# One store over the rows of two batches in an attention and gated FFN kernel

## The chip, the cores and the metric

The kernel runs on 1 core of one Trainium2 chip. The metric is the device time of one execution in microseconds (us), taken as the median of several runs. The engines are TensorE (PE, with PEld for its weight loads), VectorE (DVE), ScalarE (ACT), GpSimd (POOL) and SyncE (SP); 16 DMA engines serve the core. SP issues all loads of the attention's inputs, all DMA transposes and all stores, in one in-order queue; POOL issues the nine loads of the FFN weights.

## The reference

Causal attention over 8 batches, 8 heads and 576 positions with 16 extra "beacon" keys and values ahead of each sequence, then an FFN with a gated hidden layer over the 4608 rows of its output:

```python
k_all = np.concatenate([beacon_k, k], axis=2)        # (8, 8, 592, 64)
v_all = np.concatenate([beacon_v, v], axis=2)
scores = scale * np.matmul(q, k_all.transpose(0, 1, 3, 2))
scores = np.where(causal, -1000000000.0, scores)
a = np.exp(scores - scores.max(-1, keepdims=True))
a /= a.sum(-1, keepdims=True) + 1e-09
x = (a @ v_all).transpose(0, 2, 1, 3).reshape(4608, 512)
gate = np.maximum(x @ w_gate, 0.0)                   # w_gate, w_val: 512 x 1536
out = gate * (x @ w_val) @ w_out                     # w_out: 1536 x 512, out: 4608 x 512
```

Inputs and output are float32; the products are made in bf16 on PE.

## The kernel before

**Attention, by batch.** For each batch SP loads q, k, v and the beacons into staging tiles `st` (7 buffers, lines 520, 562 and 594 to 597). POOL scales and rounds them to bf16 (`h` at line 486, `v` at line 442), PE turns `h` with four small matmuls (line 497), and ACT or DVE copies the turned rows into `kT` and `diag`. Scores are matmuls of `diag` with `kT` (lines 655 to 663), DVE finds the row minima (line 678), ACT takes the exponential (line 689), POOL divides by the sums (line 710), a DMA transpose on SP's queue turns the probabilities (`pTb<-pb` and `pTf<-pf`, line 756), and PE multiplies them with the values (lines 766 and 795). The result goes transposed into `xT`.

**FFN, by 512 rows.** `hidden` makes the two products of line 833 for each of 12 blocks of hidden units, ACT takes the ReLU of the gate (line 837), and DVE multiplies (line 841). `project` makes one tile of 128 output rows: 12 matmuls at line 853 in three parts, a copy from PSUM to a tile `osb` (4 buffers) by ACT or DVE (lines 438 and 440), and the store on SP's queue (line 865).

**The rows that the change is about.** Each batch has 576 rows, 512 of which go through the FFN by themselves, with four stores of 128 rows. The 64 rows that remain of each batch are collected: those of batches 0 to 3 make one group, those of batches 4 to 7 another. In such a group a tile of 128 output rows holds 64 rows of one batch and 64 of the next, which lie 576 rows apart in the output. The first group is worked on in the middle of the kernel; its two tiles are stored at 236.9 and 242.0 us. The second group comes last. Its first tile is 512 columns wide, its second is made as two halves of 256 columns (`LAST_PARTS = 2`), so the last three tiles of the kernel are of this kind.

**The order of the work.** Nothing in the kernel waits by the order of the source. Every step is a task with a cost, a priority and the buffers that it holds; `Plan.order` plays the tasks through with these costs and emits them one by one, each engine's instructions in the order that the planner reached them. A DMA task has a cost of `(issue, move)`: how long it takes SP's queue to issue it and how long it takes to move. The tile framework adds the semaphores. So a task less, or another cost, can change the order of all that the planner emits after it.

Of the kernel before, what the change touches and what calls it, by code (L numbers as in the profile page):

```python
# [51 lines left out]
OUT = -1300.0  # L52
# [93 lines left out]
class Plan:  # L146
# [7 lines left out]
    def add(self, engines, cost, run, deps=(), holds=(), prio=0.0, lag=None, part=False, lazy=0.0, after=0.0, move=0.0):  # L154
        t = Task(engines if isinstance(engines, tuple) else (engines,), cost, run, deps, holds, prio, lag, part, lazy, move)
        t.ready = after
        for d in t.deps:
            d.users.append(t)
        self.tasks.append(t)
        return t  # L160
# [107 lines left out]
def kernel(  # L268
# [12 lines left out]
    nc = tc.nc  # L281
    B, H, S, D = q.shape
# [4 lines left out]
    P = 128  # L287
# [53 lines left out]
    osb_s = outs  # L341
# [7 lines left out]
    f_s, v_ps, first_ps = Share(banks, F_MOST), Share(banks, V_MOST), Share(banks, FIRST_MOST)  # L349
# [3 lines left out]
    add = plan.add  # L353


    def c_dve(n):
        return 0.07 + 0.00104 * n
# [7 lines left out]
    def c_act(n):  # L365
        return 0.06 + 0.00083 * n
# [4 lines left out]
    def c_pe(n):  # L371
        return 0.003 + n / 2400.0
# [63 lines left out]
    def copy(e, dst, src):  # L436
        if e == "ACT":
            nc.scalar.copy(dst, src)  # L438
        elif e == "DVE":
            nc.vector.tensor_copy(dst, src)  # L440
        else:
            nc.gpsimd.tensor_scalar(dst, src, 1.0, 1.0, ALU.mult, ALU.mult)
# [402 lines left out]
    def project(t0, rows, here, hT, prio, last):  # L845
        w = DM // LAST_PARTS if last else DM
        for n0 in range(0, DM, w):
            ps, osb = Hold(f_s, 4), Hold(osb_s, 1 + len(rows))
            prev = None
            for part in range(3):  # L850
                def outp(_, part=part, ps=ps, n0=n0):
                    for nf in range(4 * part, 4 * part + 4):
                        nc.tensor.matmul(ps.tile[:, :w], hT[nf].tile[:, t0:t0 + P], wo_r[:, nf, n0:n0 + w],  # L853
                                         start=(nf == 0), stop=(nf == NF - 1))

                need = [prev, weight_in["o", part]]
                for hid in here:
                    need += hid[4 * part:4 * part + 4] + (hid[:11] if part == 0 else [])
                prev = add("PE", 4 * c_pe(w), outp, need, (ps,) + tuple(hT[4 * part:4 * part + 4]),
                           prio + 0.3 + 0.01 * part + 0.001 * (n0 > 0) - (0.5 if part else 0))  # L860
            ev = add(("ACT", "DVE"), {"ACT": c_act(w), "DVE": c_dve(w)}, lambda x, ps=ps, osb=osb: copy(
                x.engine, osb.tile[:, :w], ps.tile[:, :w]), (prev,), (ps, osb), -1000 + prio)
            at = 0
            for r0, n in rows:
                add("DMA", (0.4, 0.78 * n / P), lambda _, osb=osb, r0=r0, n=n, at=at, n0=n0: nc.sync.dma_start(
                    out[r0:r0 + n, n0:n0 + w], osb.tile[at:at + n, :w]), (ev,), (osb,), prio + OUT)
                at += n


    T0 = 10.0  # L870
# [15 lines left out]
    REG = S // MT * MT  # L886
    for b in range(B):
        hT = [Hold(hid_s, len(CUTS.get(b, ())) + 1 + REG // P) for _ in range(NF)]
        cuts = [0, *CUTS.get(b, ()), REG]
        prio = 1000 + 10.0 * b  # L890
        here = []
        for a, z in zip(cuts, cuts[1:]):
            here.append(hidden(lambda ki, a=a, z=z, b=b: xT[:, ki, b * S + a:b * S + z], z - a, a, done(b, a, z), hT, prio))
            for t0 in range(a // P * P, z // P * P, P):
                project(t0, [(b * S + t0, P)], [x for x, c0, c1 in zip(here, cuts, cuts[1:]) if c0 < t0 + P and c1 > t0],
                        hT, prio, False)
            prio += 2.0
    ends = xT.rearrange("p k (b s) -> p k b s", s=S)
    for i in range(2):
        b0, b1 = i * B // 2, (i + 1) * B // 2  # L900
        w = (b1 - b0) * (S - REG)
        prio = 1000 + 10.0 * b1 - 5.0
        hT = [Hold(hid_s, 1 + w // P + (LAST_PARTS - 1) * i) for _ in range(NF)]
        deps = [x for b in range(b0, b1) for x in done(b, REG, S)]
        hid = hidden(lambda ki, b0=b0, b1=b1: ends[:, ki, b0:b1, REG:], w, 0, deps, hT, prio)
        for t0 in range(0, w, P):
            b = b0 + t0 // (S - REG)
            project(t0, [(x * S + REG, S - REG) for x in (b, b + 1)], [hid], hT, prio, i == 1 and t0 + P == w)
# [37 lines left out]
```

## Time and profile before

| | us |
|---|---|
| median of 3 runs | 409.05 (408.46 to 410.03) |
| the profiled execution | 410.43 |
| its span (first to last instruction) | 408.7 |
| PE busy | 394.1 (96%) |
| DVE, ACT, POOL busy | 315.8, 289.9, 232.7 |

Of the 42 store instructions, 32 carry 128 rows of 2 KB (256 KB), 6 carry 64 rows of 2 KB (128 KB) and 4 carry 64 rows of 1 KB (64 KB). In the profile, an instruction's line is that of the helper that recorded it: 440 and 438 are the copies of all kinds on DVE and ACT, 865 is the store. "SPq" is SP's queue of DMA issues; the time beside an issue is that of issuing, not of the transfer. "To landing" is the time from the start of the issue to the transfer's last semaphore mark.

### The profile page before, as it was taken

To read this page: it belongs to the slowest core of one execution; us is meant where nothing else is said; L and a number is where in the kernel's file an instruction comes from. 1 tells how busy PE (TensorE), PEld (TensorE's weight loads), DVE (VectorE), ACT (ScalarE), POOL (GpSimd) and SP (SyncE) were. 2 spreads that over 40 slices of the span, in tenths; PEclk is the share of its full clock that TensorE was granted. 3 is DMA by queue.
4 is the path that set the end of the run, shared out by engine and by line. 5 is a ranking of instruction groups with operands and counts; after the bars stand their busy time and mean duration, and the time that the engine had idled before them with its cause. 6 is when DMAs were issued, how large, how long until landed. Compare 5 with 4: busy or idle time off the path is not lost.

```text
span 408.7 us, 10376 instructions
## 1 busy us (share of the span) xinstructions
PE 394.1 (96%) x3276; PEld 246.8 (60%) x3311; DVE 315.8 (77%) x1159; ACT 289.9 (71%) x959; POOL 232.7 (57%) x434
## 2 busy tenths in 40 slices
PE   7899999989999999999999999999999999999994
PEld 5567867567766877555557754654554544444483
DVE  6898999889989988899998998787988544244251
ACT  6899989778888968797888799998867432033040
POOL 5899786947777667586975966875727200000000
PEclk9999999999999999999999999999999999999998
DMA  8899999999989999999999999999195730100112
GB/s 224 167 199 225 212 209 196 171 242 219 176 172 230 215 178 231 190 227 195 242 209 210 234 198 189 249 201 205 54 162 125 167 73 0 70 34 0 53 54 51
DMA packets 172616, 68.03 MB, mean 166 GB/s; under 512 B 146832, under 2 KB 168080, under 8 KB 172560
## 3 DMA queue, kind: packets, MB, share of 16 engines
q1 hardware_dynamic: 167808, 62.64, 75.5%
q0 software_dynamic: 4752, 4.72, 7.1%
q8 instruction: 26, 0.43, 0.5%
q14 instruction: 30, 0.25, 0.2%
HBM read 38.27 MB, written 9.44 MB: 117 GB/s over the span
## 4 chain that ended last, share of the span: by engine, by line
PE 84%; POOL 7%; DMA 2%; DVE 2%; ACT 2%; issue 2%; SPq 0%; POOLq 0%
PE f L833 42%; PE f L853 22%; PE f L663 7%; PE f L766 5%; PE f L497 4%; POOL xT L710 2%; POOL pb L710 2%; POOL h L486 2%; PE f L655 2%; DMA st<-in_beacon_k_dram 1%; PE f L795 1%; DMA st<-in_q_dram 1%; DVE diag L440 1%; PE f L745 1%; ACT xT L689 1%
## 5 line engine op out<-in xcount | busy, mean ns | idle before, releaser
L710 POOL TENSOR_SCALAR pb<-pb,small 128x576 bf16<-128x576 bf16 (+8 forms) x224 | 121.6, 557 | 56.0 <-DVE small L703 49.0
L689 ACT ACTIVATE pb<-f,small 128x64 bf16<-128x64 f32 (+6 forms) x256 | 131.0, 524 | 18.0 <-DVE small L678 13.1
L837 ACT ACTIVATE g<-f 128x512 f32<-128x512 f32 (+3 forms) x156 | 71.9, 470 | 67.9 <-PE f L833 66.6
L678 DVE CUSTOM_DVE_ANT_0 f<-f,mask 128x128 f32<-128x128 f32 (+7 forms) x256 | 112.0, 477 | 9.4 <-PE f L663 7.2
L833 PE MATMUL f<-xT,wv_r 128*128 128x512 bf16 (+3 forms) x616 | 111.8, 313 | 0.5
L833 PE MATMUL f<-xT,wg_r 128*128 128x512 bf16 (+3 forms) x619 | 109.5, 313 | 0.3
L841 DVE TENSOR_TENSOR hT<-g,f 128x512 bf16<-128x512 f32 (+3 forms) x156 | 80.5, 520 | 37.6 <-PE f L833 34.4
L853 PE MATMUL f<-wo_r,hT 128*128 128x512 bf16 (+1 forms) x423 | 102.0, 373 | 1.0
L833 PEld LDWEIGHTS <-wg_r 128*128 128x128 bf16 x624 | 60.0, 98 | 32.3 <-issue 0.2
L833 PEld LDWEIGHTS <-wv_r 128*128 128x128 bf16 x624 | 59.4, 98 | 33.0 <-issue 0.8
L853 PEld LDWEIGHTS <-hT 128*128 128x128 bf16 x444 | 41.6, 98 | 39.1
L689 ACT ACTIVATION_READ_ACCUMULATOR pb<-f,small 128x1 f32 x256 | 53.8, 210 | 0.0
L663 PE MATMUL f<-kT,diag 128*128 128x384 bf16 (+7 forms) x255 | 46.9, 286 | 1.9 <-DVE diag L440 0.8
L678 DVE DVE_READ_ACCUMULATOR2_ANT small<- 128x1 f32 x296 | 41.6, 141 | 0.2 <-issue 0.2
L486 POOL TENSOR_SCALAR h<-st 128x512 bf16<-128x512 f32 x62 | 37.8, 614 | 7.1 <-DMA st<-in_q_dram 2.9
L440 DVE COPY osb<-f 128x512 f32<-128x512 f32 (+1 forms) x26 | 17.6, 678 | 23.2 <-PE f L853 22.7
L710 POOL TENSOR_SCALAR xT<-xT,small 128x64 bf16<-128x64 bf16 (+4 forms) x64 | 26.9, 436 | 7.7 <-ACT xT L689 4.1
L497 PE MATMUL f<-ident,h 128*128 128x128 bf16 (+2 forms) x320 | 28.1, 217 | 2.8 <-POOL h L486 2.5
L438 ACT CAST diag<-f 64x512 bf16<-64x512 f32 (+2 forms) x52 | 23.0, 442 | 9.6 <-PE f L497 4.1
L497 PEld LDWEIGHTS <-h 128*128 128x128 bf16 (+2 forms) x320 | 20.3, 98 | 15.6 <-POOL h L486 7.9
L440 DVE CAST diag<-f 64x512 bf16<-64x512 f32 (+2 forms) x44 | 26.3, 598 | 4.2 <-ACT diag L438 2.0
L663 PEld LDWEIGHTS <-diag 128*128 128x128 bf16 x256 | 20.4, 98 | 15.0 <-issue 1.5
(67 smaller groups left out, 376.7 us busy)
## 6 DMA issues: line engine op xcount, KB each, us to landing
st<-in_q_dram SPq DMA_DIRECT2D x32, 256.0 KB, 4.5
st<-in_k_dram SPq DMA_DIRECT2D x32, 256.0 KB, 5.0
out_dram<-osb SPq DMA_DIRECT2D x32, 256.0 KB, 2.6
st<-in_v_dram SPq DMA_DIRECT2D x24, 256.0 KB, 4.7
st<-in_v_dram SPq DMA_DIRECT2D x8, 224.0 KB, 4.9
wg_r<-in_moe_w_gate_dram POOLq DMA_DIRECT2D x3, 512.0 KB, 8.5
wv_r<-in_moe_w_val_dram POOLq DMA_DIRECT2D x3, 512.0 KB, 10.3
wo_r<-in_moe_w_out_dram POOLq DMA_DIRECT2D x3, 512.0 KB, 14.2
```

The source lines that it names most:

```text
L438: nc.scalar.copy(dst, src)
L440: nc.vector.tensor_copy(dst, src)
L486: (nc.gpsimd if x.engine == "POOL" else nc.vector).tensor_scalar(to, of, by, 1.0, ALU.mult, ALU.mult)
L497: nc.tensor.matmul(to, h16.tile[:rows, a * P:(a + 1) * P], ident[:rows, :rows], start=True, stop=True)
L663: nc.tensor.matmul(view(i), t.diag.tile[:, p, j * P:j * P + P], kT[:, p, :n], start=True, stop=True)
L678: nc.vector.tensor_tensor_reduce(out=view(i), in0=view(i), in1=msk, scale=1.0, scalar=small["t"][:, 0:1] if name in "EF" else 3.0e38, op0= ...
L689: nc.scalar.activation(ph.tile.rearrange("p a n -> p (a n)")[:, a:a + n], view(i), AF.Exp, bias=small["t"][:, low:low + 1], scale=-1.0, ac ...
L710: (nc.gpsimd if x.engine == "POOL" else nc.vector).tensor_scalar(one, one, small["t"][:, 8 + i:9 + i], 1.0, ALU.mult, ALU.mult)
L833: nc.tensor.matmul(to, w_r[:, ki, nf * P:(nf + 1) * P], x, start=(ki == 0), stop=(ki == KM - 1))
L837: r = add("ACT", c_act(w), lambda _, psg=psg, g=g: nc.scalar.activation(g.tile[:, :w], psg.tile[:, :w], AF.Relu), (a,), (psg, g), -1000 + ...
L841: hid.append(add("DVE", c_dve(w), lambda _, psv=psv, g=g, nf=nf: nc.vector.tensor_mul(hT[nf].tile[:, c0:c0 + w], g.tile[:, :w], psv.tile[: ...
L853: nc.tensor.matmul(ps.tile[:, :w], hT[nf].tile[:, t0:t0 + P], wo_r[:, nf, n0:n0 + w], start=(nf == 0), stop=(nf == NF - 1))
```

## The change

A tile that holds rows of two batches is stored by one DMA instruction. The SBUF side is the whole tile of 128 partitions. The output is viewed as batch, row and column, and the destination is two batches by their last 64 rows by the columns, so its access pattern has an outer dimension of 2 and a next one of 64. `osb` is held by 2 users, the copy and the store, where it was held by 3 for these tiles. The planner is given the same cost `(0.4, 0.78)` for this store as for any store of 128 rows; it had been given two tasks of `(0.4, 0.39)`. Stores of 128 consecutive rows keep their form.

```diff
     def project(t0, rows, here, hT, prio, last):
         w = DM // LAST_PARTS if last else DM
         for n0 in range(0, DM, w):
-            ps, osb = Hold(f_s, 4), Hold(osb_s, 1 + len(rows))
+            ps, osb = Hold(f_s, 4), Hold(osb_s, 2)
...
             ev = add(("ACT", "DVE"), {"ACT": c_act(w), "DVE": c_dve(w)}, lambda x, ps=ps, osb=osb: copy(
                 x.engine, osb.tile[:, :w], ps.tile[:, :w]), (prev,), (ps, osb), -1000 + prio)
-            at = 0
-            for r0, n in rows:
-                add("DMA", (0.4, 0.78 * n / P), lambda _, osb=osb, r0=r0, n=n, at=at, n0=n0: nc.sync.dma_start(
-                    out[r0:r0 + n, n0:n0 + w], osb.tile[at:at + n, :w]), (ev,), (osb,), prio + OUT)
-                at += n
+            to = out[rows[0][0]:rows[0][0] + P, n0:n0 + w] if len(rows) == 1 else out.rearrange("(b s) d -> b s d", s=S)[
+                rows[0][0] // S:rows[0][0] // S + len(rows), REG:, n0:n0 + w]
+            add("DMA", (0.4, 0.78), lambda _, osb=osb, to=to: nc.sync.dma_start(to, osb.tile[:, :w]), (ev,), (osb,), prio + OUT)
```

In the built program the ten stores of 64 rows become five. Each engine's order is the one of before up to about 261 us of the profile shown; from there to about 320 us some instructions stand in other places, and PE's order of operations after that is the same again.

## The prediction

> **What bounds the kernel now.** I read the page first, then the table of windows, then the last microseconds of the timeline.
>
> ```profile
> PE 394.1 (96%) x3276; PEld 246.8 (60%) x3311; DVE 315.8 (77%) x1159; ACT 289.9 (71%) x959; POOL 232.7 (57%) x434
> PE 84%; POOL 7%; DMA 2%; DVE 2%; ACT 2%; issue 2%; SPq 0%; POOLq 0%
> ```
>
> PE is the bound, and the chain that ended last is mostly PE. The windows (length, then each engine's busy time, granted clock, DMA share) say how tightly:
>
> ```profile
> 238.00:250.00 12.00, 11.95 (x65) 5.81 (x64) 11.16 (x43) 10.36 (x34) 6.90 (x14) 1.00 1.06 187
> 284.00:300.00 16.00, 15.89 (x143) 8.60 (x143) 14.07 (x48) 11.39 (x38) 9.55 (x20) 1.00 0.53 96
> 403.30:406.00 2.70, 0.00 (x0) 0.00 (x0) 0.38 (x1) 0.00 (x0) 0.00 (x0) 1.00 0.69 149
> 406.00:408.70 2.70, 0.00 (x0) 0.00 (x0) 0.00 (x0) 0.00 (x0) 0.00 (x0) 0.55 0.21 46
> ```
>
> In the middle PE stands for 0.05 us in 12, so nothing can be won there, and what makes PE wait is paid in full. Ahead of 284 us the DMA engines are as full as PE (share 1.06), after it half empty. After 403.3 us PE has nothing left: the last 5.4 us are the last stores. The clock falls to half about 3 us after PE's last matmul.
>
> The timeline of those last stores:
>
> ```profile
> 402.23 3.71 SPq L865 DMA_DIRECT2D out_dram<-osb  x6
> 403.26 0.42 DVE L440 COPY osb<-f 128x256 f32<-128x256 f32 x1 [1.05 <-PE f L853]
> ```
>
> Six issues in 3.71 us: SP is still issuing 2.3 us after the last copy ends (403.68). The sixth starts at about 405.35 and lands 2.0 us later (the page's median for 64 KB), at 407.4.
>
> **What the change removes.** Three of those six issues, 0.6 us each. The last store could then be issued at about 403.75 instead of 405.35. If a merged store moves like the others, it lands 2.0 to 2.4 us later, at 405.8 to 406.1: 1.3 to 1.6 us are won. In the middle, two issues of 0.6 us leave SP's queue (at 237.5 and 242.7); a transpose is next each time, but PE doesn't wait for it, so that is worth nothing.
>
> **What it adds: another shape of transfer.** Every DMA of the trace posts 16 landing marks of 4 bytes (for two stores the DMA view has 288 packets: 256 rows and 32 marks), so each is spread over 16 engines. All have, on both sides, an outermost dimension of 16, 48, 64, 80, 112 or 128 rows, which 16 divides. The merged store has 128 partitions on one side and 2 batches of 64 rows on the other. No row shows how that is cut. The bounds are 16 parts, as all others, and 2, the only parts that both outermost dimensions have in common. I take 2: cutting along the outermost dimension explains each of the transfers seen, and in the destination that dimension is 2.
>
> The Trainium skill, "DMA: Bandwidth & Descriptors", section "Why a DMA increments its semaphore by 16 and not by 1", says that for such DMAs the largest number up to 16 that divides the slowest dimension of both sides is taken, on the lowest-numbered engines. By it all five merged stores go over the same two engines; by the marks alone, which are always 16 here, the sum would be the gain of 1.3 to 1.6 us. No run here has yet shown a transfer of fewer than 16 parts.
>
> **Its price per row.** From the DMA view, of 357 to 361 us (two stores of 128 rows alone) and of 405.2 to 408.7 us (three stores of 64 rows of 1 KB):
>
> ```profile
> q1 hardware_dynamic: 288, 0.52, 35.4%
> out_dram<-osb SPq DMA_DIRECT2D x1, 256.0 KB, 2.0
> q1 hardware_dynamic: 240, 0.20, 26.2%
> ```
>
> 35.4% of 4 us is 1.42 us on each engine for 16 rows: 88 ns for 2 KB. 26.2% of 3.5 us is 0.92 us for 12 rows: 76 ns for 1 KB. For 1 KB the lower bound is half of 88, 44 ns. A store of 128 rows lands 2.0 us after its issue, of which 8 rows are 0.7 us; 1.3 us are fixed.
>
> **The end.** First merged store: issue at 402.23, 1.3 us fixed, 64 rows on each of two engines at 88 ns are 5.6 us: 409.1. I take equal shapes to go to equal engines, so the two halves queue behind it: 128 rows at 44 to 76 ns, 5.6 to 9.7 us: 414.8 to 418.9. Against 407.4 that is +7.4 to +11.5. I take +8.5: 88 ns for 2 KB was had with all 16 engines writing, so two alone should be near 44 ns for 1 KB. Should two engines move rows a third faster than all of these, it is +3.7.
>
> **The middle.** SP's queue, then POOL and the chain:
>
> ```profile
> 236.88 1.19 SPq L865 DMA_DIRECT2D out_dram<-osb  x2
> 242.05 1.22 SPq L865 DMA_DIRECT2D out_dram<-osb  x2
> 244.76 4.45 SPq L756 DMA_TRANSPOSE pTb<-pb  x1
> 250.44 0.58 SPq L520 DMA_DIRECT2D st<-in_q_dram  x1
> 256.22 0.61 POOL L486 TENSOR_SCALAR h<-st 128x512 bf16<-128x512 f32 x1
> 257.40 0.22 PE f L497 x4
> ```
>
> Each merged store puts 56 more rows on two engines: 4.9 us at 88 ns, 9.9 us for both. The transposes and loads behind them in the same queue are spread over all 16 engines, and each is complete only when those two have done their part. What the engines' gaps take up, the DMA view of 236.8 to 250 us tells (busy tenths in slices of 0.33 us):
>
> ```profile
> DMA  4001979789999999999997979911999900099999
> GB/s 88 0 0 37 223 174 217 144 166 219 210 218 217 216 216 220 216 221 201 226 171 155 298 158 213 209 23 33 213 261 203 78 2 9 10 251 291 289 291 290
> ```
>
> After the first four slices some six are empty: 2.0 us. Some of the rest runs at 215 GB/s, some at 290; work that has piled up may go at the faster rate and regain up to 2 us of 8 us of transposes. The lag at 250 us is thus 5.9 to 7.9 us; I take 5.9. The load of q at 250.44 lands after 4.9 us (median of that window), at 255.3. POOL takes it up at 256.22, which leaves a cover of 0.9 us, and PE turns it at once. So PE stands still for 5.0 us at line 497; behind it wait all of PE's instructions, and later loads only keep the lag. The transposes lose as much, but the values need the last one (about 252) at 263.
>
> A stall over 3 us may also lose the clock, as at 406 us. At the start eleven 128x256 matmuls took 2.51 us, later 1.36; the slow pace held from 1.9 to about 5.8 us, so regaining it costs up to 2 us. I take 1.
>
> **The new order.** From 261 us the planner's order differs, but PE's operations come in the same turns from about 317 us, and the idle time it could win or lose in between is 0.7 us in 106 us before: nothing, within 0.7.
>
> **Sum.** 8.5 + 5.0 + 1.0 = +14.5 us. The profiled execution would take 410.43 + 14.5 = 424.9; the median of the runs lies 1.38 below it: 423.5 us.
>
> **Rivals.**
> 1. *Cut into 16 as ever* (the other side): the end is 1.3 to 1.6 us earlier and the middle unchanged, 407.6 us. For it: 16 marks on every transfer seen. The same page's table of advice, which prefers one 128-partition transfer to two halves, would give this too. Against it: a destination whose outer dimension is 2. It decides from about eight engines on: then each has 16 rows of every store, 1.4 us and twice 0.7 to 1.2 us, which from 403.5 on end at 406.3 to 407.3, no later than 407.4. Chance 0.13.
> 2. *Two engines, but the middle is covered*: store rows slip between the transposes' packets and POOL finds its tile in time. Only the end counts: 417.5 us. For it: share 1.06 counts packets that wait beside each other, so the engines may have more room than it looks. Against it: the cover is 0.9 us. Chance 0.20.
> 3. *Two engines, and rows take twice as long in company*, or SP's queue itself stops until they drain: the lag is 9.9 more, 433 us. For it: the issue of a transpose took 4.45 us at 244.76, with traffic, and 3.70 at 308.35, without. Chance 0.12.
>
> **Numbers.** The forecast has 0.55. The range runs from 412.7 (rows a third faster, middle covered) to 433 (stall 12, end +11.5); it leaves out rival 1 and about half of rival 3, 0.19. A measurement of this kernel tells about 0.5%, 2 us, from no change. Rival 1 gives 0.03 faster and 0.08 same; in the remaining 0.02 of it the new order loses over 3.5 us, and that is slower, as are all other cases: 0.89.
>
> **What would show it.** In the changed profile: three issues at the end, the landing of the first of them about 7 us after its issue instead of 2.4, the last landing 8.5 us later after PE's last matmul than now; two landing marks from the DMA engines for a merged store; a gap of PE at line 497 near 257 us, put down to POOL `h`, and a lower clock after it. Landings of 2.4 us would prove me wrong on the cut, PE without a gap on the middle.

## The result: 15.45 us slower

The changed kernel takes 424.99 us (median of 6 runs), the kernel before 409.54 us beside it: a ratio of 1.0377, 95% interval 1.035 to 1.0404. The ratios here and below leave out executions far off the others: two of the ten of the first experiment, at 822.0 and 2307.1 us, which its median of 409.36 us still counts (409.26 without them). The profiled execution has a span of 423.2 us against 408.7.

The page of the changed kernel, busy times and the chain:

```profile
PE 395.5 (93%) x3276; PEld 247.0 (58%) x3311; DVE 314.9 (74%) x1157; ACT 290.7 (69%) x961; POOL 232.8 (55%) x434
PE 80%; POOL 7%; issue 3%; DVE 3%; DMA 2%; ACT 2%; SPq 0%; POOLq 0%; DVEq 0%
```

PE has the same work, 1.4 us longer; its share fell because the span grew around it. Two places of the timeline show where. SP's queue in the middle, then what POOL and PE do with the loads (in brackets the idle time before, and what ended it):

```profile
234.74 0.67 SPq L865 DMA_DIRECT2D out_dram<-osb  x1
235.52 7.89 SPq L756 DMA_TRANSPOSE pTb<-pb  x1
243.50 0.54 SPq L865 DMA_DIRECT2D out_dram<-osb  x1
246.49 7.48 SPq L756 DMA_TRANSPOSE pTb<-pb  x1
255.20 0.58 SPq L520 DMA_DIRECT2D st<-in_q_dram  x1
257.74 0.61 POOL L442 TENSOR_SCALAR v<-st 80x512 bf16<-80x512 f32 x1 [6.29 <-DMA st<-in_v_dram]
261.07 0.61 PE L497 MATMUL f<-ident,h 128*128 128x128 bf16 x4 [5.81 <-POOL h L486]
```

This execution had come to the first of these stores 2.14 us earlier than that of before, with the same instructions up to there; times are compared from the first merged store on. Issuing the two transposes takes 7.89 and 7.48 us instead of 3.78 and 4.45. The load of q is issued 20.46 us after the first store instead of 13.56, and PE stands for 5.81 us at line 497. The windows around that gap, and the end:

```profile
255.20:261.10 5.90, 0.09 (x2) 0.03 (x2) 1.54 (x11) 0.47 (x1) 3.36 (x8) 0.73 1.11 264
261.10:266.00 4.90, 4.85 (x17) 2.16 (x19) 0.69 (x1) 2.84 (x8) 4.69 (x8) 0.62 1.18 225
412.00:423.20 11.20, 0.00 (x0) 0.00 (x0) 0.00 (x0) 0.00 (x0) 0.00 (x0) 0.63 0.12 41
```

In the gap the granted clock falls, and it stays low for most of the 4.9 us after it: the records have half clock from 257.95 to 264.78, of which PE worked 3.7 us, so 1.85 us are lost. At the end nothing computes for 11.2 us. SP's last three issues and the last copy, and the DMA view of 408.5 to 423.2 us:

```profile
408.60 5.16 SPq L865 DMA_DIRECT2D out_dram<-osb  x3
409.63 0.42 DVE L440 COPY osb<-f 128x256 f32<-128x256 f32 x1 [1.06 <-PE f L853]
DMA  0000111201011111111111111111111111110000
GB/s 0 0 0 22 11 28 28 45 6 39 33 45 45 56 45 56 56 45 56 45 56 45 50 45 50 50 45 50 47 47 50 50 45 50 50 39 0 0 0 0
DMA packets 390, 0.52 MB, mean 36 GB/s; under 512 B 6, under 2 KB 262, under 8 KB 390
```

Three stores of 128 rows are 384 rows; the other 6 packets are their landing marks, two for each store, where the stores of the kernel before have 16 each. About a tenth of the 16 engines is busy, at some 50 GB/s, for 12 us. The third issue alone lasts 3.68 us, where the six of before took 0.6 us each: SP is held up in handing it over. From the first of these issues to the last landing it is 13.44 us, before 5.16.

### The profile page after: what moved, and what is told of

It is laid out like the page before. It is cut to its first block, busy times and chain, and to the rows that moved or that the text cites. A ratio compares the mean times of both kernels' runs of the same rounds, so it can differ in the third digit from the quotient of the medians.

```text
span 423.2 us, 10376 instructions
## 1 busy us (share of the span) xinstructions
PE 395.5 (93%) x3276; PEld 247.0 (58%) x3311; DVE 314.9 (74%) x1157; ACT 290.7 (69%) x961; POOL 232.8 (55%) x434
## 4 chain that ended last, share of the span: by engine, by line
PE 80%; POOL 7%; issue 3%; DVE 3%; DMA 2%; ACT 2%; SPq 0%; POOLq 0%; DVEq 0%
PE f L833 40%; PE f L853 21%; PE f L663 6%; PE f L766 5%; PE f L497 4%; POOL xT L710 2%; DMA st<-in_q_dram 2%; POOL pb L710 2%; PE f L655 1%; POOL h L486 1%; PE f L795 1%; DVE diag L440 1%; POOL v L442 1%; PE f L658 1%; ACT diag L438 1%
## 5 line engine op out<-in xcount | busy, mean ns | idle before, releaser
L442 POOL TENSOR_SCALAR v<-st 128x512 bf16<-128x512 f32 (+1 forms) x38 | 23.3, 615 | 12.1 <-DMA st<-in_v_dram 11.5
```

## The experiments

Times are medians; the kernel before had 408.73 us beside the runs of the order alone, the end alone, the middle alone and the rows in turn in PE's operand, and 408.89 us beside the others.

**The order alone.** The planner's tasks and order of the changed kernel, with two stores of 64 rows issued by each task:

```diff
-            add("DMA", (0.4, 0.78), lambda _, osb=osb, to=to: nc.sync.dma_start(to, osb.tile[:, :w]), (ev,), (osb,), prio + OUT)
+
+            def store(_, osb=osb, to=to, n0=n0):
+                if len(rows) == 1 or False:
+                    nc.sync.dma_start(to, osb.tile[:, :w])
+                else:
+                    for i, (r0, n) in enumerate(rows):
+                        nc.sync.dma_start(out[r0:r0 + n, n0:n0 + w], osb.tile[n * i:n * i + n, :w])
+
+            add("DMA", (0.4, 0.78), store, (ev,), (osb,), prio + OUT)
```

> The planner's tasks, costs, holds and order of the changed kernel, but each of its five merged stores is issued as two stores of 64 rows. If the cut over two engines is the cause, nothing of the loss is left: 409.5 us, within 0.7 (the idle time of PE that the order could touch). If the new order or the shorter hold of the buffer costs time, that part of the 15.5 us stays; if it were all of it, 425.

409.36 us, ratio 1.001 (0.9998 to 1.0022). The new order and the shorter hold cost nothing that is measured here (at most 0.9 us by the interval); the loss lies in the five store instructions.

**The end alone, the middle alone.** The same, with merged stores for one group of tiles:

```diff
-                if len(rows) == 1 or False:
+                if len(rows) == 1 or rows[0][0] // S >= B // 2:   # the end; "<" for the middle
```

> As the run with two issues, but the three tiles of the last group go by merged stores. By the cut over two engines only the end is longer, by the 8.3 us that the two traces differ in from the first of these stores on: 417.8 us, PE without a gap near 255 us. If the loss of the middle hangs on the order and not on the stores, the gap is there and the time is 425.

> As the run with two issues, but the two tiles of the first group go by merged stores. By the cut over two engines PE stands still for 5 to 6 us at line 497 and runs at half clock for a while after it, and the end is as before: 409.5 + 8.5 = 418 us. The parts of the two runs should add up to the 15.5 us of the change. If the middle were covered, 409.5.

416.87 us for the end (ratio 1.02, 1.0187 to 1.0213), 416.16 us for the middle (1.0184, 1.0171 to 1.0197): +8.1 and +7.4 us, together 15.5, as much as the change. PE's waits at line 497 (in all, times, longest) with the end alone, then with the middle alone:

```profile
PE f L497 <- POOL h L486: 1.0, 3, 0.6
PE f L497 <- POOL h L486: 7.7, 6, 5.6
```

**Is it the outer dimension?** The kernel before, with late stores of 128 rows written in another order of rows within the same 128 consecutive rows, so that the output's rows are exchanged. Each batch has four, with an outer dimension of 2, 4, 8 and 16:

```diff
                 add("DMA", (0.4, 0.78 * n / P), lambda _, osb=osb, r0=r0, n=n, at=at, n0=n0: nc.sync.dma_start(
-                    out[r0:r0 + n, n0:n0 + w], osb.tile[at:at + n, :w]), (ev,), (osb,), prio + OUT)
+                    out[r0:r0 + n, n0:n0 + w] if n < P or r0 // S < B - 2 else out[r0:r0 + n, :].rearrange(
+                        "(a s) d -> s a d", a=64 >> r0 % S // P), osb.tile[at:at + n, :w]), (ev,), (osb,), prio + OUT)
```

> The kernel before, in which the eight late stores of 128 rows (those of batches 6 and 7, when no other transfer is under way) go to the same 128 consecutive output rows in another order of the rows, so that the destination's outer dimension is 2, 4, 8 and 16 for the four tiles of a batch; the rows are then not where the reference has them. If the outer dimension sets the number of engines, the landings are 1.3 us fixed and 64, 32, 16 and 8 rows at 88 to 101 ns: about 7 to 8, 4.1 to 4.5, 2.7 to 2.9 and 2.0 to 2.1 us, and the DMA engines' marks are 3, 5, 9 and 16. If two far regions make the merged stores slow, or the count is not tied to that dimension, all land in about 2.0 us.

The DMA view of 349.5 to 365 us, which holds one batch's four stores:

```profile
GB/s 0 0 0 11 26 58 42 32 21 21 58 32 63 53 53 58 63 74 111 122 106 122 143 201 259 317 159 90 90 95 48 32 32 37 37 26 26 26 5 0
DMA packets 543, 1.07 MB, mean 69 GB/s; under 512 B 30, under 2 KB 30, under 8 KB 542
```

Of the 543 packets 512 are rows, one belongs to an instruction load, and 30 are marks: 2 + 4 + 8 + 16, where four such stores had 64. Each store's semaphore rises one time more than that where the count is under 16 (3, 5, 9 and 16 times, as expected); that one rise comes 1.0 us after the start of the issue, long before the rows are through. So the count follows the destination's outer dimension, with the rows all in one region. The landings were as expected for the first store alone: 8.0, 12.2, 9.1 and 8.9 us after their issues, against 7 to 8, 4.1 to 4.5, 2.7 to 2.9 and 2.0 to 2.1. The expectation had left out that the four queue behind each other, which fits engines of the first store that are among those of every other. Its rows and those of the next three, 64 + 32 + 16 + 8 = 120 on each of two engines, took from 351.0 to 364.4 us, 111 ns for a row. The time, one run of 409.05 us, shows no loss: nothing waits for these stores.

This is the count that the Trainium skill's page "DMA: Bandwidth & Descriptors" gives in "Why a DMA increments its semaphore by 16 and not by 1", the largest number up to 16 that divides both slowest dimensions; the marks agree for 2, 4, 8 and 16.

**Merged, with an outer dimension of 64.** The two batches' rows stand in turn on the partitions, in PE's operand:

```diff
-                    if len(x.shape) == 3:
-                        to = to.rearrange("p (b s) -> p b s", b=x.shape[1])
+                    if len(x.shape) == 4:
+                        to = to.rearrange("p (c s b) -> p c s b", c=x.shape[1], b=2)
...
-            to = out[rows[0][0]:rows[0][0] + P, n0:n0 + w] if len(rows) == 1 else out.rearrange("(b s) d -> b s d", s=S)[
-                rows[0][0] // S:rows[0][0] // S + len(rows), REG:, n0:n0 + w]
+            to = out[rows[0][0]:rows[0][0] + P, n0:n0 + w] if len(rows) == 1 else out.rearrange("(b s) d -> s b d", s=S)[
+                REG:, rows[0][0] // S:rows[0][0] // S + len(rows), n0:n0 + w]
...
-        hid = hidden(lambda ki, b0=b0, b1=b1: ends[:, ki, b0:b1, REG:], w, 0, deps, hT, prio)
+        hid = hidden(lambda ki, b0=b0, b1=b1: ends[:, ki, b0:b1, REG:].rearrange("p (c b) s -> p c s b", b=2), w, 0, deps, hT, prio)
```

> Merged stores as in the changed kernel, to the same two regions of the output, but the rows of the two batches stand in turn on the partitions of the tile (the hidden layer's operand is read in that order), so that the destination's dimensions are 64 by 2 instead of 2 by 64. By the cut, 64 is shared out over 16 engines: landings of 2 to 2.4 us, the end shorter by the three issues that are gone, 1.3 to 1.6 us: 408.1 us. If it is the two regions, or one instruction for both, that makes these stores slow, 425.

433.15 us, ratio 1.0613 (1.0586 to 1.064), and yet no sign of slow stores: each posts 16 marks, the last three land 2.42, 2.10 and 2.10 us after their issues, and the end from first issue to last landing is 3.58 us instead of 5.16. The loss is a new one, on PE. The same eight matmuls in the kernel before, then in this run:

```profile
392.61 1.04 PE L833 MATMUL f<-xT,wv_r 128*128 128x256 bf16 x8
406.82 2.11 PE L833 MATMUL f<-xT,wv_r 128*128 128x256 bf16 x8
```

From one such group to the next it is 0.87 us before and 1.95 us here, 109 and 243 ns a matmul: the operand is now read one bf16 element at a time, the next one 1152 bytes away. 192 matmuls of this kind are 25.7 us more; less the 1.58 us won at the end that is 24.1, and the time is 24.4 us longer. The two far regions and the one instruction for both are the same as in the changed kernel, so neither of them is what makes its stores slow.

**The same, with the turn made by DVE.** PE reads as before; DVE writes the hidden layer's columns in the other order:

```diff
+        pairs = len(rhs(0).shape) == 3
+        turned = (lambda x: x.rearrange("p (c s b) -> p c b s", b=2, s=S - REG)) if pairs else (lambda x: x)
+        natural = (lambda x: x.rearrange("p (c b s) -> p c b s", b=2, s=S - REG)) if pairs else (lambda x: x)
...
-                hT[nf].tile[:, c0:c0 + w], g.tile[:, :w], psv.tile[:, :w]), (r, b_), (psv, g, hT[nf]), -1000 + prio))
+                turned(hT[nf].tile[:, c0:c0 + w]), natural(g.tile[:, :w]), natural(psv.tile[:, :w])), (r, b_), (psv, g, hT[nf]), -1000 + prio))
...
```

The store is written as in the run before.

> As the run with the rows in turn, merged stores with a destination of 64 by 2, but the order of the rows is made where DVE writes the hidden layer, so that PE reads its operand in the order of before. The stores should land in 2.1 to 2.4 us and the end should be shorter by 1.6 us, as in that run; PE's matmuls of 256 columns should be back at 109 ns. 407.2 us against 408.8 of the kernel before, 0.4% faster. If DVE's writes in steps of two elements cost more than it has spare at the end, up to 1 us of that is lost.

407.74 us, ratio 0.9976 (0.996 to 0.9992): 1.15 us less than the kernel before. That is 0.3%, and clear of no change only by the interval: the kernel before itself had medians of 409.54, 408.73 and 408.89 us at three times. DVE's product and SP's end:

```profile
397.16 0.44 DVE L844 TENSOR_TENSOR hT<-g,f 128x256 bf16<-128x256 f32 x1 [0.41 <-PE f L836]
401.27 2.02 SPq L868 DMA_DIRECT2D out_dram<-osb  x3
402.30 0.42 DVE L440 COPY osb<-f 128x256 f32<-128x256 f32 x1 [1.06 <-PE f L856]
```

The stores' side is as in the run before. PE's groups of eight matmuls follow each other at 0.87 us again. The product takes 0.44 us where it took 0.41. Three issues in 2.02 us end 0.57 us after the last copy; before it was six in 3.71 and 2.26 us after. First issue to last landing is 3.58 us. This is the gain the merged store can give. That the median gained 1.15 us and not 1.58 was not followed up.

**Does the place matter?** Merged stores of the first group, held back behind the last transpose and load:

```diff
-            add("DMA", (0.4, 0.78), store, (ev,), (osb,), prio + OUT)
+            add("DMA", (0.4, 0.78), store, (ev,), (osb,), prio + OUT,
+                after=330.0 if len(rows) > 1 and rows[0][0] // S < B // 2 else 0.0
```

> Merged stores in the first group only, as in the run with the middle alone, but held back until after 330 us of the planner's time, behind the last transpose and load; the end goes by two issues. If the middle's 7.4 us are paid by what is queued behind these stores, they are gone: 409 us, within 1 for the other order, although the two stores still take 7 us and more to land. If a store over two engines costs its time wherever it stands, 416.

409.1 us, ratio 1.0009 (0.9992 to 1.0025). The DMA view of 329 to 350 us has the two stores going as slowly as in the changed kernel:

```profile
GB/s 4 4 27 35 55 51 51 51 82 51 51 51 51 55 51 51 51 51 51 51 55 35 0 0 0 0 0 0 0 0 0 0 0 0 0 0 0 0 0 0
```

Some 10 us at 51 GB/s, which on two engines is 80 ns for a row of 2 KB, and PE's wait at line 497 is 1.0 us in all. A slow store that nothing waits for costs nothing; in the middle what is queued behind it pays, at the end the kernel itself.

**Whose queue stands still?** The same stores at their time, issued by ACT:

```diff
-            add("DMA", (0.4, 0.78), store, (ev,), (osb,), prio + OUT)
+            if len(rows) > 1 and rows[0][0] // S < B // 2:
+                add("ACT", 0.1, lambda _, osb=osb, to=to, n0=n0: nc.scalar.dma_start(to, osb.tile[:, :w]), (ev,), (osb,), -2000 + prio, 12.0)
+            else:
+                add("DMA", (0.4, 0.78), store, (ev,), (osb,), prio + OUT)
```

> Merged stores in the first group only, at the time when their tiles are ready, but issued by ACT instead of SP; the end goes by two issues. If the loss of the middle comes from SP's own queue standing still while the store's rows drain, SP's transposes keep their issue times of 3.8 to 4.5 us and most of the 7.4 us is gone: 410 to 412 us, with 0.6 us of ACT's time for each issue. If two of the engines simply lack the time for 112 more rows, the transposes are as late as before and the time is 416.

414.66 us, ratio 1.0162 (1.0118 to 1.0205), which can't be told from the 1.0184 of the same stores on SP's queue. The first expectation fell. The outcome is the second one's, a late transpose and about 416 us, but its reason, two engines that lack the time, isn't the whole of it. The trace is of the longest of the four executions, 419.49 us; the others had 413.95 to 414.80. DMA views: 2 us of the kernel before with a transpose alone (240 to 242 us), the same stretch of the changed kernel (stores on SP's queue), and the first merged store of the changed kernel from its first row to its last (236 to 242.15 us):

```profile
DMA packets 1686, 0.43 MB, mean 216 GB/s; under 512 B 1686, under 2 KB 1686, under 8 KB 1686
DMA packets 50, 0.10 MB, mean 51 GB/s; under 512 B 0, under 2 KB 0, under 8 KB 50
DMA packets 598, 0.38 MB, mean 62 GB/s; under 512 B 470, under 2 KB 470, under 8 KB 598
```

From this run, stores on ACT's queue: the DMA view of 240 to 243 us, the two queues from 244 to 251.5 us (q1 is SP's, q10 ACT's), and two of SP's issues:

```profile
DMA packets 447, 0.20 MB, mean 67 GB/s; under 512 B 399, under 2 KB 399, under 8 KB 447
q1 hardware_dynamic: 1296, 0.32, 120.1%
q10 hardware_dynamic: 161, 0.33, 11.1%
235.34 8.66 SPq L756 DMA_TRANSPOSE pTb<-pb  x1
249.96 4.10 SPq L520 DMA_DIRECT2D st<-in_q_dram  x1
```

On SP's queue nothing but the store's rows moves in the 2 us: 50 rows, and not one of a transpose's packets, on any engine. The queue behind the store doesn't stop at once: over the whole drain 470 small packets pass beside its 128 rows, and 469 beside those of the second store; undisturbed, 470 are through in 0.6 us (1686 in 2 us). If fourteen engines share them evenly, each runs some 33 packets ahead and then stands; that is an estimate, since the trace doesn't name the engine of a packet.

With the store on ACT's queue the small packets keep moving, but slowly: 399 beside 48 rows in 3 us, and 1296 beside 161 packets of the stores (rows and two marks) in 7.5 us. That is 81 on each of 16 engines, if they are spread evenly, and 80 on each of the store's two. It fits two engines that serve rows and small packets alike while the other fourteen are held to their pace. Issuing the transpose beside the store takes 8.66 us (3.78 before, 7.89 in the changed kernel), and the load of q behind it 4.10 us (0.58 in both). The Trainium skill's page "DMA: Bandwidth & Descriptors" says, under "Queues, rings and completion order", that an engine takes packets from its queues in turn, a packet there being typically 9 to 17 descriptors. The equal counts agree with turns of equal length; how long one turn is they don't show.

## Why the prediction was right, and where its steps were off

- **The cut.** Two parts of 64 rows, as forecast: two marks a store, and a count that follows the outer dimension in the runs with 2, 4, 8 and 16. (Not every DMA of the kernel before posts 16 marks, as the prediction has it: its trace has 4625 records of 4 bytes for 242 DMA instructions, 16 for a load or a store and 32 for each of the 47 transposes.)
- **Price per row.** Taken: 88 ns for 2 KB, and near 44 of 44 to 76 ns for 1 KB. At the end the first store's 64 rows took from 409.80 to its marks at 416.27, 101 ns a row; the marks of the next two follow at 2.72 us each, 42 ns a row. The 101 ns include a slow start, which no run explains; in the run with the late stores, past their start, it is 80 ns.
- **The end.** Forecast +8.5, measured +8.3 in the traces and +8.1 with the end alone. That it is so close is in part luck, as two misses nearly cancel: the first store's rows took 0.8 us more than at 88 ns, and the two halves took 5.4 us where +8.5 allows them 6.7 (the 5.6 us of +7.4, and 1.1 more).
- **The middle's stall.** Forecast 5.0 us at line 497, put down to POOL `h`; found 5.81, there and so named. But the step before it, "The transposes and loads behind them in the same queue are spread over all 16 engines, and each is complete only when those two have done their part", had the wrong picture. I had the issues on time and two engines late. In fact the queue behind the store comes to a stand on all 16 engines after some 470 packets, and the lag is in SP's issues: the load of q is issued 6.9 us late. From that issue to PE's start at line 497 it is 5.9 us, and PE's wait is 1.1 us less than the lag (a cover of 0.9 was forecast). That the lag came near the 5.9 us forecast is in part luck: the two stores' rows took 6.1 and 6.5 us to drain, 12.6 in all, and how all but 6.9 us of that was made up was not worked out. One part of the forecast's working is borne out: after the store the piled-up transposes ran at 290 GB/s (242.5 to 244.5 us), against 216 in the kernel before (240 to 242 us). Rival 3 had this mechanism ("SP's queue itself stops until they drain") with twice the price.
- **The clock.** Taken 1.0 us, measured 1.85.
- **The sum.** 14.5 forecast, 15.45 measured. The middle is the term that was too small: 7.4 us with the middle alone, against 6.0; stall and clock in the changed kernel's trace are 5.8 + 1.85 = 7.7. Between the two single traces the middle differs by 8.5 us, and the 0.8 more were not traced to a cause.
- **The order.** Nothing within 0.7 us, forecast and found.
- **The gain that was buried.** 1.3 to 1.6 us for the three issues: 1.58 at the end of the run with DVE's turn.
- **Rivals.** The cut into 16 (1) and the covered middle (2) fell: the middle alone costs 7.4 us. Whether eight engines would do, as rival 1 had it, was not tried at the end of the kernel.

## What to carry to other kernels

Before two stores are made one, write down the outermost dimension of both sides: three issues fewer at the end were worth 1.58 us here, and an outer 2 cost 7 to 8 us at each of the two places. Put a dimension that 16 divides outermost, if need be by turning the rows where an engine with time to spare writes them, and not where PE reads them. A slow transfer is paid for by what waits for it, the end of the kernel or what is queued behind it; another queue didn't help, and where nothing waited the same stores were free.

## What the runs showed that I had not expected

A transfer on two engines brings the whole of the queue behind it to a stand after some 470 packets, also the part that would run on the other fourteen; from another queue it lets small packets pass at the pace of its rows, 133 to 173 a microsecond where 843 went before. And a matmul whose moving operand is read one bf16 element at a time, 1152 bytes from one to the next, takes 243 ns for 256 columns instead of 109.
